# Attention output formed transposed in quadrants of 32 rows, denominator sums shared by three engines, and a new order of steps

## The chip, the cores and the metric

The kernel runs on one core of a Trainium2 chip. The metric is the device time of one execution in microseconds (us). A run more than 1.5% above the fastest of the same kernel is called slow, and only fast runs are compared. A profile gives the span, from the first instruction to the last, and this is 1.8 us shorter than the device time of the same execution, for both kernels.

## The reference, cut to what matters

A gated linear attention over 768 positions feeds a dense layer with a rational activation.

```python
# batch 4, heads 8, positions 768, head size 48; d_model 384, d_ff 2048
f = 1 / (1 + exp(-f_logit))
for t in range(S):
    state = f[t][:, None] * state + outer(k[t], v[t])
    y[t] = q[t] @ state
x = y.transpose(0, 2, 1, 3).reshape(3072, 384)      # heads side by side
h = x @ w_in                                         # 384 x 2048
P = a0 + a1*h + a2*h**2 + a3*h**3
Q = 1 + abs(b0)*abs(h) + abs(b1)*h**2
out = (P / (Q + 1e-6)) @ w_out                       # 2048 x 384
```

## The kernel before

The work is cut into 12 units of 256 rows (two batches, 128 positions). The dense part of a unit has two groups, a and b, each a tile of 128 x 2048. A list of tokens, `STEPS`, fixes the order in which the steps are put into the engines' streams; each engine's stream holds them in that order, and the traces show it kept: before, ScalarE runs `efl:4` at 63.50 us and `efl:3` behind it at 66.02, though unit 3's gates were issued first (52.2 and 58.0). `efl:3` is the gate exponential and logarithm of unit 3, `y:3` its attention output, `xe:3` the copy that leaves it as `xT` (features on partitions), `ha0:3` half of the first dense product of group a, `za`, `qa` (absolute value, square), `ua`/`Ua` the sum of the two, `La` the logarithm of the denominator, `Ea` its exponential, `ga` the quotient, `oa` and `Oa` the second product and its way out. Of the attention part, `mk` and `mq` are VectorE's products with k and q, `T` and `Te` the transposes of these and the copy that leaves them as `qkT`, `sc` the scores, `m` their mask; of the dense part, `ta` and `Ba` are VectorE's first steps of the numerator (tiles `t` and `pb`).

The attention output comes with positions on partitions, so a scaled copy and six transposes a unit stand between it and the dense product:

```python
def a_y(n):
    y = psA.tile([C, 2, 512], F32, name="y", tag="A")
    ...
    if s["c"] > 0:
        for j, p, i in heads:                        # 16 heads of the unit
            r = slice(64 * i, 64 * i + D)
            mm(j, p, i, s["qkT"][r, j, 0, p, :], s["st"][r, j, p, :])     # 48 columns
    for j, p, i in heads:
        mm(j, p, i, s["scm", j][:, i * HP + p, :], s["vn"][:, j, 2 * p + i, :])

def a_ye(n):
    nc.scalar.activation(ysb..., s["y"]..., AF.Copy, scale=sig[:, 0:1])
def a_x(n):
    for j in range(UB):
        for kk in range(KD):
            nc.tensor.transpose(xps[:, j, kk, :], s["ysb"][:, j, kk * P:(kk + 1) * P], ident)
def a_xe(n):
    nc.scalar.copy(xTs[n].rearrange("p k b t -> p b k t"), s["xps"])
```

The sum of the denominator is formed by TensorE for 22 of the 24 groups, by adding with an identity matrix, and by VectorE for two; the sums of the numerator go by accumulating DMA for 18 groups:

```python
P_BY_DMA = {4, 5, 6, ..., 21}
def m_u(n, half):                                    # tokens ua0, ua1, ub0, ub1
    for i, src in enumerate((s["h2"], s["z"])):
        for e in range(2):
            nc.tensor.matmul(u[:, e, :], ident, src[:, ...], start=(i == 0), stop=(i == 1))
def m_add_u(n):                                      # tokens Ua, Ub
    nc.vector.tensor_add(s["u"], s["z"], s["h2"])
```

The loads are issued by the sync engine and GpSimd. Two pieces of `w_in` come as fp32 through the sync queue (`wst`) and are cast by GpSimd; the rest of the weights come by GpSimd's queue. A tiny copy (`after`) makes the sync queue wait until weights have landed (9.2 us for `w_in`, 18.1 us for `w_out` before), so that loads of later units are issued after them:

```python
def load_w_in(g, dma_cast=True):
    src = moe_w_in[:, cols].rearrange("(ko ki) n -> ki ko n", ki=P)       # 128 partitions
    ...
load(0)
casts = [load_w_in(0, False), load_w_in(1, False)]
load(1)
...
def after(n):
    src = (w_in_sb[0:1, 0, d_ff - 16:d_ff], w_out_sb[0:1, KF - 1, 0:16])[n]   # the last pieces
    nc.sync.dma_start(out=hold[0:1, n, :], in_=src)
after(0)
load(2)
nc.gpsimd.tensor_copy(hold[0:1, 2, :], at_[2]["qn"][0:1, UB - 1, H - 1, 0:16])
load_v(2)
for g in range(KF // WB):
    load_w_out(g)
after(1)
for token in STEPS.split():
    ...
    if key == "mk" and n + 3 < NUN:
        load(n + 3)
```

Of the kernel before, what the change touches and what calls it, by code (L numbers as in the profile page):

```python
# [8 lines left out]
F32 = mybir.dt.float32  # L9
# [9 lines left out]
    efl:0 cs:0 A1:0 A0:0 mk:0 mq:0 T:0 sv:0 Te:0 sc0:0 m0:0 sc1:0 m1:0 y:0 al:0 ye:0 st:0 efl:1 x:0 cs:1  # L19
    xe:0 ha1:0 A1:1 A0:1 mk:1 mq:1 ha0:0 Ya1:0 Ya0:0 sv:1 T:1 ta:0 Te:1 qa:0 hb0:0 sc0:1 Yb0:0 m0:1 al:1  # L20
    hb1:0 Yb1:0 sa:0 sc1:1 m1:1 y:1 efl:2 ye:1 Bb:0 cs:2 A1:2 st:1 za:0 Ba:0 ua0:0 mk:2 A0:2 La0:0 ua1:0
    La1:0 vl:3 x:1 tb:0 mq:2 xe:1 T:2 zb:0 qb:0 ha1:1 Te:2 Ea:0 sb:0 sv:2 Pa:0 Ya1:1 ha0:1 efl:4 sc0:2
    m0:2 ub0:0 Ya0:1 efl:3 ta:1 sc1:2 al:2 hb0:1 m1:2 ga:0 Lb0:0 y:2 qa:1 Yb0:1 cs:3 A0:3 st:2 A1:3
    ub1:0 za:1 Ba:1 ye:2 Pb:0 hb1:1 x:2 Lb1:0 vl:4 Yb1:1 mk:3 qb:1 mq:3 xe:2 ha1:2 Bb:1 cs:4 Eb:0 T:3
    Ya1:2 A0:4 A1:4 ua0:1 tb:1 Te:3 zb:1 sv:3 La0:1 efl:5 sc0:3 ua1:1 sa:1 ha0:2 La1:1 Ya0:2 gb:0 oa0:0
    al:3 m0:3 sc1:3 hb0:2 sb:1 m1:3 qa:2 hb1:2 y:3 mk:4 vl:5 Ea:1 Yb0:2 Yb1:2 ub1:1 ye:3 za:2 ub0:1
    oa1:0 Lb1:1 mq:4 ta:2 Pb:1 st:3 T:4 Te:4 Lb0:1 ua0:2 Eb:1 ua1:2 sc0:4 x:3 La0:2 xe:3 Pa:1 Oa:0 m0:4
    cs:5 sv:4 La1:2 al:4 sc1:4 Ba:2 ga:1 sa:2 ob0:0 A1:5 ha0:3 m1:4 qb:2 A0:5 ha1:3 tb:2 mq:5 Ea:2 y:4
    Ya0:3 Ya1:3 Bb:2 st:4 zb:2 ye:4 efl:6 mk:5 gb:1 za:3 hb0:3 ob1:0 Yb0:3 x:4 ub1:2 T:5 hb1:3 Te:5
    Lb1:2 qa:3 Pa:2 ub0:2 Ob:0 xe:4 Yb1:3 Lb0:2 sv:5 vl:7 ha0:4 sc0:5 ta:3 al:5 Eb:2 Ba:3 Ya0:4 sb:2  # L30
    m0:5 oa0:1 ha1:4 sc1:5 ga:2 Pb:2 sa:3 ua1:3 efl:7 Ya1:4 La1:3 oa1:1 ua0:3 Oa:1 La0:3 cs:6 zb:3 m1:5
    A0:6 Pa:3 ob0:1 tb:3 qb:3 gb:2 A1:6 hb1:4 Bb:3 ob1:1 Ea:3 vl:6 Yb1:4 ub0:3 sb:3 qa:4 mk:6 y:5 Ob:1
    Ba:4 Lb0:3 ub1:3 oa0:2 cs:7 Lb1:3 mq:6 ye:5 A0:7 A1:7 za:4 hb0:4 st:5 oa1:2 T:6 ta:4 ga:3 mk:7 Te:6
    Yb0:4 Eb:3 zb:4 ua1:4 Oa:2 Pb:3 ua0:4 x:5 La1:4 mq:7 La0:4 sc0:6 ob0:2 m0:6 ob1:2 xe:5 ha1:5 Bb:4
    sv:6 sc1:6 sa:4 ha0:5 Ea:4 tb:4 qb:4 Ya1:5 al:6 ub1:4 m1:6 efl:8 sb:4 Pa:4 Ya0:5 y:6 hb0:5 Lb1:4
    gb:3 ye:6 st:6 Ob:2 hb1:5 T:7 Yb0:5 cs:8 Pb:4 za:5 ta:5 Yb1:5 x:6 A0:8 qa:5 ub0:4 oa0:3 Te:7 vl:8
    xe:6 Lb0:4 Ba:5 A1:8 oa1:3 sc0:7 Eb:4 ua1:5 ga:4 qb:5 m0:7 sa:5 ua0:5 Pa:5 Bb:5 sc1:7 La1:5 sv:7
    vl:9 La0:5 efl:9 ha0:6 al:7 m1:7 Ya0:6 ha1:6 zb:5 Ya1:6 gb:4 mq:8 Oa:3 y:7 ye:7 tb:5 hb0:6 mk:8 cs:9
    ob0:3 st:7 qa:6 T:8 Yb0:6 A0:9 hb1:6 A1:9 Ea:5 x:7 Te:8 sb:5 za:6 sc0:8 Yb1:6 vl:10 ob1:3 ta:6 ub0:5
    xe:7 m0:8 Lb0:5 Ba:6 sv:8 sa:6 mk:9 ub1:5 sc1:8 al:8 Ob:3 Lb1:5 m1:8 Pb:5 ua0:6 Pa:6 Eb:5 ga:5 oa0:4  # L40
    La0:6 ua1:6 gb:5 y:8 La1:6 mq:9 oa1:4 efl:10 qb:6 tb:6 ha1:7 zb:6 ha0:7 st:8 vl:11 Oa:4 Ya1:7 ob0:4
    ye:8 Ya0:7 sb:6 Bb:6 Pb:6 Ea:6 ub1:6 T:9 ob1:4 za:7 Lb1:6 hb1:7 Te:9 x:8 qa:7 sc0:9 Ob:4 ub0:6 Yb1:7
    ta:7 m0:9 sa:7 xe:8 hb0:7 ga:6 Lb0:6 sc1:9 cs:10 Yb0:7 oa0:5 m1:9 Ba:7 Pa:7 ua1:7 A1:10 zb:7 mk:10
    tb:7 A0:10 mq:10 qb:7 Eb:6 La1:7 ha1:8 sv:9 Ya1:8 y:9 al:9 ha0:8 ua0:7 oa1:5 ye:9 Ya0:8 gb:6 La0:7
    T:10 ub0:7 Bb:7 Oa:5 ob0:5 Te:10 za:8 Ea:7 Lb0:7 ub1:7 sb:7 efl:11 Lb1:7 sc0:10 ob1:5 Ob:5 hb1:8
    st:9 m0:10 Yb1:8 Ba:8 Eb:7 hb0:8 oa0:6 ta:8 qa:8 sc1:10 Yb0:8 cs:11 A0:11 ga:7 Pb:7 gb:7 x:9 oa1:6
    m1:10 A1:11 ua0:8 ua1:8 mk:11 xe:9 La0:8 zb:8 qb:8 y:10 La1:8 ye:10 ha0:9 sa:8 tb:8 ha1:9 mq:11 Oa:6
    Ya0:9 x:10 Ya1:9 Bb:8 ob0:6 sb:8 ta:9 za:9 ub1:8 ob1:6 Ea:8 ub0:8 Lb1:8 Lb0:8 qa:9 Pa:8 hb0:9 Yb0:9
    T:11 Pb:8 Ba:9 hb1:9 xe:10 Ob:6 Te:11 ua0:9 Yb1:9 sc0:11 Eb:8 oa0:7 sa:9 oa1:7 m0:11 La0:9 Pa:9
    ua1:9 ga:8 La1:9 sc1:11 qb:9 Oa:7 tb:9 ha1:10 Ea:9 zb:9 m1:11 ha0:10 y:11 Bb:9 Ya1:10 Ya0:10 ye:11  # L50
    ob0:7 ub0:9 sb:9 ub1:9 x:11 gb:8 Lb0:9 ta:10 ob1:7 Lb1:9 Ob:7 za:10 hb1:10 hb0:10 qa:10 oa0:8 Ba:10
    sa:10 Eb:9 ga:9 Yb1:10 Yb0:10 tb:10 ua0:10 xe:11 La0:10 ua1:10 oa1:8 La1:10 zb:10 qb:10 Oa:8 ha1:11
    Pb:9 Ya1:11 Pa:10 ha0:11 gb:9 ob0:8 ob1:8 sb:10 ub1:10 Ya0:11 Bb:10 Ea:10 za:11 Ob:8 qa:11 ub0:10
    Lb1:10 ta:11 Lb0:10 Eb:10 Pb:10 oa0:9 Ba:11 sa:11 hb1:11 Pa:11 oa1:9 hb0:11 ga:10 Yb1:11 Ua:11 Oa:9
    ob0:9 Yb0:11 ob1:9 gb:10 La0:11 qb:11 Bb:11 Ob:9 zb:11 Ea:11 Ub:11 tb:11 sb:11 ga:11 oa0:10 oa1:10
    Lb0:11 Oa:10 ob0:10 Pb:11 ob1:10 Eb:11 Ob:10 gb:11 oa0:11 oa1:11 Oa:11 ob0:11 ob1:11 Ob:11
# [3 lines left out]
P_BY_DMA = {4, 5, 6, 7, 8, 9, 10, 11, 12, 13, 14, 15, 16, 17, 18, 19, 20, 21}  # L60

TE_ON_ACT = frozenset()
O_ON_DVE = frozenset()
# [3 lines left out]
def kernel(  # L67
# [60 lines left out]
    qkp = [consts.tile([C, UB, 2, H, 64], BF16, name=f"qkp{i}") for i in range(NQK)]  # L128
    lsp = [consts.tile([C, UB, H, 64], BF16, name=f"lsp{i}") for i in range(NQK)]
    states = [consts.tile([P, UB, HP, D], BF16, name=f"state{u}") for u in range(NU)]  # L130
# [21 lines left out]
    def load_v(n):  # L152
        at_[n]["vn"] = ld.tile([C, UB, H, D], BF16, name="vn")
        rows(nc.gpsimd, at_[n]["vn"], v, n)
# [6 lines left out]

    def a_ef(n):
        s = at_[n]
        fl = "p b h d -> p (b h d)"
        ef = at.tile([C, UB, H, D], F32, name="ef")
        nc.scalar.activation(ef.rearrange(fl), s["fn"].rearrange(fl), AF.Exp, scale=-1.0)  # L166
# [17 lines left out]
    def a_mul(n, i):  # L184
        s = at_[n]
        nc.vector.tensor_mul(s["qk"][:, :, i, :, 0:D], s[("qn", "kn")[i]], s["A", i])  # L186

    def a_T(n):
        s = at_[n]
        tp = psA.tile([P, UB, 2, HP, C], BF16, name="tp", tag="A")  # L190
        for j in range(UB):
            for i in range(2):
                for p in range(HP):
                    nc.tensor.transpose(tp[:, j, i, p, :],  # L194
                                        s["qk"][:, j, i, 2 * p:2 * p + 2, :].rearrange("t h d -> t (h d)"),
                                        ident)
# [12 lines left out]
    def a_sv(n):  # L209
# [8 lines left out]
        for j in range(UB):  # L218
            for p in range(HP):
                nc.tensor.matmul(s["al"][:, j * HP + p:j * HP + p + 1],  # L220
                                 s["ls"][:, j, 2 * p:2 * p + 2, :].rearrange("t h d -> t (h d)"),
# [338 lines left out]
```

## Time and profile before

| | before |
|---|---|
| time, median of 2 runs | 268.51 us (268.48 to 268.55) |
| span of the profiled run | 265.7 us (device time 267.52) |
| busy: TensorE, VectorE, ScalarE | 229.0, 215.7, 206.5 us |
| granted TensorE clock, mean | 0.949 |
| first dense VectorE operation | 29.95 us |
| VectorE from there to its last operation | 227.5 us, of which 203.2 busy and 24.4 idle |
| tail after it | 8.2 us |

Read the table from the bottom. From its first dense operation on, VectorE has a fixed amount of work; the end moves only if that stream starts earlier, has fewer holes, or has less in it.

### The profile page before, as it was taken

How to read it: one execution, taken by the hardware profiler on the slowest of the kernel's cores; microseconds unless marked ns; L12 is line 12 of the kernel's file. 1: busy time of each engine (PE TensorE's matmuls, PEld its weight loads, DVE VectorE, ACT ScalarE, POOL GpSimd, SP SyncE). 2: the span in 40 equal slices, each digit the busy share in tenths (PEclk: the TensorE clock that was granted, in tenths of full speed). 3: DMA queues.
4: the chain of work that ended last, by engine and by line, in shares of the span. 5: the costliest groups of instructions: out<-in, count | busy, mean ns of one | idle time of the engine just before them, and what ended most of it. 6: DMA issues, size and time to landing. Idle time of an engine off the chain costs nothing.

```text
span 265.7 us, 5413 instructions
## 1 busy us (share of the span) xinstructions
PE 229.0 (86%) x2263; PEld 153.3 (58%) x2263; DVE 215.7 (81%) x237; ACT 206.5 (78%) x225; POOL 49.1 (18%) x61
## 2 busy tenths in 40 slices
PE   6659947500879999999999999999999999999884
PEld 2334726300557567666677685777667667776542
DVE  6260799300999999999999999999899889789970
ACT  3306586104999999999999998989999889989861
POOL 5080039000200022141022433211010211110000
PEclk9986997955799999999999999999999999999999
DMA  9999659999995649699999299952350852624111
GB/s 115 267 218 170 107 75 139 181 173 188 185 172 94 120 90 133 137 161 189 202 202 171 54 172 223 153 110 40 71 110 1 171 112 70 140 57 109 59 59 59
DMA packets 109975, 34.94 MB, mean 131 GB/s; under 512 B 100992, under 2 KB 106880, under 8 KB 109952
## 3 DMA queue, kind: packets, MB, share of 16 engines
q0 software_dynamic: 30464, 14.16, 42.0%
q1 hardware_dynamic: 79200, 20.45, 40.9%
q8 instruction: 17, 0.28, 0.4%
q14 instruction: 6, 0.05, 0.1%
q10 hardware_dynamic: 288, 0.00, 0.1%
HBM read 25.17 MB, written 4.72 MB: 112 GB/s over the span
## 4 chain that ended last, share of the span: by engine, by line
PE 67%; DMA 13%; SPq 7%; ACT 5%; POOL 4%; issue 2%; DVE 0%; ACTq 0%
PE hp L320 21%; PE op L419 20%; PE u L354 13%; SPq L159 7%; DMA w_in_sb<-in_moe_w_in_dram 4%; DMA w_out_sb<-in_moe_w_out_dram 3%; PE y L260 3%; PE tp L194 3%; PE sc L240 2%; DMA wst<-in_moe_w_in_dram 2%; DMA qn<-in_q_dram 2%; DMA kn<-in_k_dram 2%; ACT qi L372 1%; POOL vn L159 1%; PE xps L301 1%
## 5 line engine op out<-in xcount | busy, mean ns | idle before, releaser
L320 PE MATMUL hp<-xT,w_in_sb 128*128 128x256 bf16 x576 | 71.1, 277 | 18.4 <-ACT y L334 15.8
L320 PEld LDWEIGHTS <-w_in_sb 128*128 128x128 bf16 x576 | 56.2, 99 | 28.9 <-issue 19.0
L419 PE MATMUL op<-w_out_sb,gall 128*128 128x384 bf16 x368 | 66.2, 326 | 2.0 <-ACT osb L200 1.3
L334 ACT CAST y<-hp 128x1024 bf16<-128x1024 f32 x48 | 48.4, 1016 | 10.2 <-PE hp L320 9.7
L419 PEld LDWEIGHTS <-gall 128*128 128x128 bf16 x384 | 36.7, 98 | 26.5 <-issue 1.8
L367 ACT ACTIVATE lq<-u,sig 128x1024 f32<-128x1024 f32 x44 | 48.4, 1119 | 4.2 <-PE u L354 3.4
L372 ACT ACTIVATE qi<-lq 128x2048 bf16<-128x2048 f32 x24 | 46.2, 1925 | 0.1
L391 POOL DMA_DIRECT2D t<-pb x18 | 16.4, 910 | 134.3 <-DVE t L382 113.9
L377 DVE TENSOR_SCALAR t<-y,a_sb 128x2048 bf16<-128x2048 bf16 x24 | 20.1, 837 | 18.9 <-ACT y L334 18.8
L249 DVE TENSOR_TENSOR scm<-sc,mask 128x1024 bf16<-128x1024 f32 x24 | 29.3, 1220 | 3.4 <-PE sc L240 3.4
L402 DVE TENSOR_TENSOR gall<-t,qi 128x2048 bf16<-128x2048 bf16 x24 | 29.2, 1219 | 1.0 <-ACT qi L372 0.9
L339 DVE TENSOR_TENSOR h<-y 128x2048 bf16<-128x2048 bf16 x24 | 29.2, 1217 | 0.4 <-ACT y L334 0.4
L382 DVE TENSOR_TENSOR t<-t,h 128x2048 bf16<-128x2048 bf16 x24 | 29.2, 1218 | 0.0
L159 POOL DMA_DIRECT2D vn<-in_v_dram x24 | 23.9, 1045 | 27.4 <-PE y L260 27.4
L354 PE MATMUL u<-h,ident 128*128 128x512 bf16 x88 | 26.2, 380 | 0.6 <-ACT A L180 0.6
L354 PE MATMUL u<-z,ident 128*128 128x512 bf16 x88 | 26.2, 379 | 0.5 <-DVE z L344 0.5
L354 PEld LDWEIGHTS <-ident 128*128 128x128 bf16 x176 | 16.3, 98 | 16.9 <-issue 1.6
L166 ACT ACTIVATE ef<-fn 128x768 f32<-128x768 f32 x12 | 10.2, 854 | 19.9 <-DMA fn<-in_f_logit_dram 19.9
L180 ACT ACTIVATE A<-cs 128x768 f32<-128x768 f32 x24 | 18.4, 820 | 2.8 <-PE cs L173 2.8
L385 DVE TENSOR_SCALAR pb<-y,a_sb 128x2048 bf16<-128x2048 bf16 x24 | 20.3, 845 | 0.0
L186 DVE TENSOR_TENSOR qkp<-kn,A 128x768 bf16<-128x768 f32 x12 | 11.4, 951 | 10.1 <-ACT A L180 7.0
L344 DVE TENSOR_SCALAR z<-y 128x2048 uint16<-128x2048 uint16 x24 | 17.3, 721 | 0.9 <-ACT y L334 0.9
(59 smaller groups left out, 226.8 us busy)
## 6 DMA issues: line engine op xcount, KB each, us to landing
t<-pb POOLq DMA_DIRECT2D x18, 512.0 KB, 5.3
fn<-in_f_logit_dram SPq DMA_DIRECT2D x24, 192.0 KB, 4.4
kn<-in_k_dram SPq DMA_DIRECT2D x24, 192.0 KB, 4.6
qn<-in_q_dram SPq DMA_DIRECT2D x24, 192.0 KB, 4.9
out_dram<-osb SPq DMA_DIRECT2D x24, 192.0 KB, 2.0
vn<-in_v_dram POOLq DMA_DIRECT2D x24, 96.0 KB, 5.7
wst<-in_moe_w_in_dram SPq DMA_DIRECT2D x2, 768.0 KB, 6.1
w_out_sb<-in_moe_w_out_dram POOLq DMA_DIRECT2D x4, 384.0 KB, 7.5
```

What stands on the lines that cost most here:

```text
L159: eng.dma_start(out=dst[:, j], in_=src[u * UB + j, :, c * C:(c + 1) * C, :].rearrange("h t d -> t h d"))
L249: nc.vector.tensor_mul(m, s["sc", j].rearrange("s i p t -> s (i p) t"), mb)
L320: nc.tensor.matmul(hp[:, e, :], w_in_sb[:, kk, f * P:(f + 1) * P], xT[:, kk, :], start=(kk == 0), stop=(kk == KD - 1))
L334: nc.scalar.copy(part_of(tile_of(n, "y"), half), mg[n]["hp", half].rearrange("p a n -> p (a n)"))
L339: nc.vector.tensor_mul(s["h2"], s["y"], s["y"])
L354: nc.tensor.matmul(u[:, e, :], ident, src[:, (half * 2 + e) * NB:(half * 2 + e + 1) * NB], start=(i == 0), stop=(i == 1))
L367: nc.scalar.activation(lq if whole else part_of(lq, half), s["u"] if whole else s["u", half].rearrange("p a n -> p (a n)"), AF.Ln, scale=s ...
L372: nc.scalar.activation(part_of(tile_of(n, "qi"), part, parts), part_of(mg[n]["lq"], part, parts), AF.Exp, scale=-1.0)
L382: nc.vector.tensor_mul(s["t"], s["t"], s["h2"])
L385: nc.vector.tensor_scalar(tile_of(n, "pb"), mg[n]["y"], a_sb[:, 1:2], a_sb[:, 0:1], op0=ALU.mult, op1=ALU.add)
L402: nc.vector.tensor_mul(galls[m][:, lo:lo + w, :].rearrange("p a n -> p (a n)"), part_of(s["t"], part, parts), part_of(s["qi"], part, parts))
L419: nc.tensor.matmul(ops[m, b], galls[m][:, mm, b * C:(b + 1) * C], w_out_sb[:, mm, :], start=(mm == 0), stop=(mm == KF - 1))
```

## The change

The intent: form the attention output already transposed, so that the copy `ysb` and the transposes `x` go; take the sums of the denominator off TensorE, mostly to accumulating DMA; give eight copies of `qkT` to ScalarE in exchange; and search a new order that knows how long the first loads take.

Each matmul of the new output writes into one quadrant of 32 rows. Two heads of 48 rows fill three quadrants, and the middle one gets 16 rows of each. Heads 0 to 3 go to partitions 0 to 63 and heads 4 to 7 to partitions 64 to 127. The rows of `xT` thereby stand in another order than the features of the reference, and the rows of `w_in` must stand in the same one; each piece of `w_in` is therefore loaded by two transfers of 64 partitions.

```diff
 # attention output: features on partitions, in quadrants
-        y = psA.tile([C, 2, 512], F32, name="y", tag="A")
+        y = psA.tile([P, KD, UB, C], F32, name="y", tag="A")
+        cols = {(1, 1): (0, 32), (0, 0): (ZC, ZC + 32), (1, 2): (32, 64), (0, 1): (ZC + 32, 64)}
+        def mm(j, p, i, quad, lhsT, rhs):
+            lo, hi = cols[p % 2, quad]
+            qd = 3 * (p // 2) + quad
+            r = 64 * i + 32 * (qd % 2)
+            nc.tensor.matmul(y[r:r + hi - lo, qd // 2, j, :], lhsT[:, lo:hi], rhs, ...)
+        todo = [(j, p, i, quad) for j in range(UB) for half, quad in cols
+                for p in range(half, HP, 2) for i in range(2)]
...
-    def a_ye(n):
-    def a_x(n):
 def a_xe(n):
-        nc.scalar.copy(xTs[n].rearrange("p k b t -> p b k t"), s["xps"])
+        nc.scalar.activation(xTs[n], s["y"], AF.Copy, scale=sig[:, 0:1])
 # sums
-P_BY_DMA = {4, 5, 6, ..., 21}                                # 18
+P_BY_DMA = {5, 7, 8, 10, 11, 13, ..., 20, 21, 22}             # 15
+U_BY_DMA = {3, 7, 8, 9, 10, 12, 13, 14, 17, 19, 21, 23}       # 12; 6 on TensorE, 6 on VectorE
-TE_ON_ACT = frozenset()
-O_ON_DVE = frozenset()
+TE_ON_ACT = {0, 1, 2, 4, 5, 7, 8, 11}
+O_ON_DVE = {(4, 0), (10, 0)}
 def m_add_u(n):
+        if n in U_BY_DMA:
+            nc.gpsimd.dma_start(out=s["u"], in_=s["h2"], accum_op=ALU.add)
 # loads of the head
-        src = moe_w_in[:, cols].rearrange("(ko ki) n -> ki ko n", ki=P)
+        src = [moe_w_in[i * DM // 2:(i + 1) * DM // 2, cols].rearrange("(ko ki) n -> ki ko n", ki=P // 2)
+               for i in range(2)]
...
-            nc.sync.dma_start(out=t, in_=src)
+            for i in range(2):
+                nc.sync.dma_start(out=t[i * P // 2:(i + 1) * P // 2], in_=src[i])
...
+    for t in vpd + states:
+        nc.gpsimd.memset(...)                                 # five tiles
-        src = (w_in_sb[0:1, 0, d_ff - 16:d_ff], w_out_sb[0:1, KF - 1, 0:16])[n]
+        src = (w_in_sb[0:1, 0, 3 * WB * P - 16:3 * WB * P], w_out_sb[0:1, 3 * WB - 1, 0:16])[n]
-    nc.gpsimd.tensor_copy(hold[0:1, 2, :], at_[2]["qn"]...)
+    nc.gpsimd.tensor_copy(hold[0:1, 2, :], at_[2]["kn"]...)
 # order: all of STEPS is new; in the first lines
-    ... sc0:0 m0:0 sc1:0 m1:0 y:0 al:0 ye:0 st:0 efl:1 x:0 cs:1 xe:0 ha1:0 ... efl:4 sc0:2 ... efl:3 ...
+    ... sc0:0 m0:0 efl:1 sc1:0 m1:0 y:0 xe:0 st:0 cs:1 A0:1 A1:1 ha0:0 mk:1 mq:1 ha1:0 ... za:0 ... efl:3 ... efl:4 ...
```

The layouts of the tiles that hold q, k, the gates, v and the state were changed to fit; loads of unit n + 3 now wait in program order for the third of the three reads of unit n. The diff also has fewer dummy matmuls on zeros, which keep TensorE busy in the head: 31 for 47.

## The prediction

> **What bounds the kernel now.** I read the slices of the page first. The columns are 40 equal slices of 6.64 us; the digits are tenths busy, and PEclk is the granted clock.
>
> ```profile
> PE   6659947500879999999999999999999999999884
> DVE  6260799300999999999999999999899889789970
> ACT  3306586104999999999999998989999889989861
> PEclk9986997955799999999999999999999999999999
> ```
>
> Three regimes show: a head in which all engines are part idle, a hole in slices 9 and 10 (53 to 66 us) in which TensorE and VectorE are at 0 and the clock falls to 0.5, and a long middle with every engine at 9. Next the list of waits over the whole run (total us, times, longest), and the sync engine's own:
>
> ```profile
> ACT ef L166 <- DMA fn<-in_f_logit_dram: 19.9, 2, 16.3
> DVE t L377 <- ACT y L334: 18.8, 3, 16.2
> PE hp L320 <- ACT y L334: 15.8, 1, 15.8
> SPq L492 <- DMA w_out_sb<-in_moe_w_out_dram: 18.1, 1, 18.1
> ```
>
> The first three are one event. The timeline of that place gives its cause (start us, length us):
>
> ```profile
> 51.63 0.50 SPq L492 DMA_DIRECT2D hold<-w_out_sb  x1
> 52.23 2.26 SPq L159 DMA_DIRECT2D fn<-in_f_logit_dram  x2
> ...
> 58.03 1.75 SPq L159 DMA_DIRECT2D fn<-in_f_logit_dram  x2
> ...
> 63.50 0.84 ACT L166 ACTIVATE ef<-fn 128x768 f32<-128x768 f32 x1 [16.28 <-DMA fn<-in_f_logit_dram]
> ...
> 66.17 2.72 PE L320 MATMUL hp<-xT,w_in_sb 128*128 128x256 bf16 x12 [15.80 <-ACT y L334]
> ```
>
> The sync queue issues in order. It stands on "after(1)", a tiny copy that waits for the last piece of w_out, until 51.6; only then come the loads of unit 3 (52.2) and unit 4 (58.0). And the order has `efl:4` ahead of `efl:3`, so ScalarE waits for the later of the two, and with it everything else. Then the stretches (us, busy of each engine, clock, DMA share, GB/s) say what binds once the stream runs:
>
> ```profile
> 110.00:150.00 40.00, 40.00 (x417) 26.61 (x412) 40.00 (x43) 38.15 (x43) 8.67 (x10) 1.00 0.97 156
> 150.00:190.00 40.00, 40.00 (x458) 28.54 (x457) 38.91 (x43) 37.73 (x44) 10.31 (x11) 1.00 0.87 132
> 190.00:230.00 40.00, 40.00 (x372) 27.04 (x370) 37.64 (x40) 36.89 (x38) 5.12 (x6) 1.00 0.44 96
> ```
>
> TensorE is at 40.00 of 40, VectorE at 94 to 100%, ScalarE at 92 to 95%. Two engines bind together, so relieving TensorE alone is worth only what VectorE leaves idle: 40.00 − 37.64 = 2.4 us of the last window. I take VectorE as the measure: its first operation of the dense stage is at 29.95 (`ta:0`), its last at 257.47, which is 227.5 us. It is busy 215.66 − 12.55 (before 30 us) = 203.1 of them and idle 24.4: 16.2 in the hole, 8.2 elsewhere. 265.7 − 257.5 = 8.2 us of tail follow.
>
> [...] 16 transposes with 128 columns advance the chain by 0.89 us, 56 ns each; 32 y matmuls with 48 columns by 0.81 us, 25 ns each. [...] In the trace two row tiles do run side by side: 8 score matmuls of 128 columns span 0.40 us, of which one alone takes 0.218, so 26 ns a step against 56. Quadrants of 32 columns are not in this trace. [...]
>
> **The change part by part.** The durations are from these groups (busy us, mean ns):
>
> ```profile
> L354 PE MATMUL u<-h,ident 128*128 128x512 bf16 x88 | 26.2, 380 | 0.6 <-ACT A L180 0.6
> L393 DVE TENSOR_TENSOR t<-t,pb 128x2048 bf16<-128x2048 bf16 x6 | 7.3, 1218 | 0.0
> L200 DVE COPY qkT<-tp 128x2048 bf16<-128x2048 bf16 x12 | 14.7, 1222 | 3.9 <-PE tp L194 3.9
> L276 ACT ACTIVATE ysb<-y,sig 128x768 bf16<-128x768 f32 x12 | 11.0, 914 | 5.5 <-PE y L260 5.5
> L367 ACT ACTIVATE lq<-z,sig 128x2048 f32<-128x2048 bf16 x2 | 4.0, 2006 | 0.0
> ```
>
> *TensorE.* The identity sums u fall from 22 groups to 6. One group is 8 matmuls of 512 columns, 8 × 0.216 = 1.73 us in the chain (4 take 0.86), so −16 × 1.73 = −27.7 us. The 72 transposes x go: 72 × 56 ns = −4.0. The new y has 64 matmuls of 128 columns a unit (32 in the two first units) for 32 of 48 columns: at the 25 ns [...], 704 instead of 352, +8.8 us. Sum −22.9. Without any overlap they would cost 56 ns, +30, and the sum would be −1.
>
> *VectorE.* Sums u on it: 2 to 6, +4 × 1.22 = +4.9. Sums of t and pb on it: 6 to 9, +3.7. Eight of the twelve qkT copies leave: −9.8. Two output copies come, about 0.5 each (the 384-element state product takes 0.552): +1. Sum −0.2: nothing.
>
> *ScalarE.* [...] The twelve ysb go: −11.0; xT now reads fp32 with a pointer, 0.914 for 0.814: +1.2. Logarithms: 12 halves at 1.119 and 18 whole at 2.006 for 44 and 2: −3.7. Two output copies: −1.0. Sum +0.6 on 206.5.
>
> *DMA.* Twelve sums u and 15 of t: 27 accumulating transfers of 512 KB for 18. From 190 to 240 us, with no loads, the share sums to 21.9 us of all engines for 7 of them and the output stores, so at most 3.1 us each; nine more are at most 28 us over some 170, or 0.16 on a share of 0.9.
>
> *The head.* Both holds now wait for the third piece of four, and the one on GpSimd for kn instead of qn. I estimate the w_in hold 2 us sooner (27.8 to about 25.5), the kn gate another 2, and one piece of w_out, a fourth of the 11.5 us from 40.1 to 51.6, 2.9: unit 3's loads issue about 45 instead of 52.2, and fn is there 4.4 us later, near 50. Its reader is now the right one, `efl:3`, and comes later: by my count in program order 34.5 us of ScalarE work stand before it, against 22.6 before the old `efl:4`. With xT of unit 0 at 21.5 to 22 and 27.5 us of ScalarE work from there (× 0.94, as successive durations overlap: summed durations 218.9, busy 206), ScalarE cannot be there before 47.5, and VectorE (25.9 us of work in the same order, × 0.93, from 26.5) comes to that place at 50.6. So the hole shrinks to 0 to 3 us. Unit 0 itself loses the ysb step and the transposes: before, y ends at 20.1, xT at 24.1, the first hp is at 25.6. Without ysb and x (3.2 us), [...] hp starts near 22.5 and the first dense VectorE operation (`za:0`) near 26.5 instead of 29.95. It matters because VectorE has one unbroken stream from there.
>
> *Sum.* Start 26.5; VectorE work 203.1 × (220.4 ÷ 219.4 of summed durations left) = 204; idle 9, of which 2 while few jobs are ready, 4 in the middle and 3 at the end, where the last sum u (`Ub:11`) goes by DMA and ScalarE then does logarithm, exponential in series; tail 8.2. Span 247.7. Timed runs lie 2.8 over the span (268.5 − 265.7): 250.5. I call it 251.
>
> **The rivals.**
> 1. *The hole moves rather than closes.* If the loads of units 3 and 4 still come late (GpSimd now clears five tiles before it loads v of unit 0, and issues two more descriptor batches of 0.77 us each for w_in), 3 to 8 us of idle stay: 254 to 259. For it: the chain of waits runs through these very DMAs for its first 65 us. Against it: the order was searched with load times.
> 2. *DMA becomes the bound.* Share already reaches 1.49 between 73 and 80 us; a sum that took 5.3 us (4.5 to 7.3) may take 10, and ScalarE's logarithm now waits for it. Worth 0 to 8 us: up to 259. Against it: shares over 1 in the old middle cost VectorE nothing.
> 3. *The y quadrants run one after another.* Then TensorE is where it was (−1 us), still with VectorE at its side: the middle keeps its 6 us of idle, and I get 254. So this mechanism hardly decides the time.
> 4. *Better than said.* TensorE no longer binding, the idle of 180 to 250 us goes fully and the tail tightens: 245 to 247.
>
> **Range and chances.** The sum is 251; a closed hole and an unbroken middle make 246, one of the first three rivals 254 to 259, two of them 262. I give 245 to 259 8 times in 10. Same would need 263 or more, which needs the hole back in most of its size: 0.03. Slower would need the new transfers to break the middle: 0.01.
>
> **What would show it.** Right: ScalarE's wait for fn under 4 us in one piece; no empty slice after the fourth; first z near 26.5; VectorE busy 213 to 218, ScalarE 204 to 211; TensorE under 82% of the span, 48 u matmuls left in place of 176, y matmuls some 25 ns apart or less. Wrong: a wait over 5 us on fn, kn or w_out; a wait of the logarithm on an accumulating DMA over 3 us in total; landing times of sums above 8 us; VectorE idle over 6 us in the middle; VectorE busy above 220.

## The result, and the profile after

| | before | after |
|---|---|---|
| time, median of 2 runs | 268.51 us | 253.78 us (253.5 to 254.06) |
| span of the profiled run | 265.7 | 252.3 |
| mean granted clock | 0.949 | 0.946 |
| busy: TensorE, VectorE, ScalarE | 229.0, 215.7, 206.5 | 207.8, 213.6, 207.6 |
| first dense VectorE operation | 29.95 | 33.77 |
| VectorE busy, idle from there to its last operation | 203.2, 24.4 | 202.3, 7.9 |
| tail | 8.2 | 8.35 |

The ratio is 0.9451, with a 95% interval of 0.9406 to 0.9497. A ratio here is the mean time of one kernel's fast runs over the mean of the other's fast runs of the same rounds, so it is not quite the ratio of the medians that are quoted. The kernel is faster by 5.5%. The span is 1.8 us shorter than the device time of the same execution, for both kernels.

First the slices of the kernel after, columns as in the prediction, 6.31 us each:

```profile
PE   8667366946988898887998969989999999997754
DVE  7122168899999999999999999979999999999940
ACT  2425427799899999998996999998999899999841
PEclk9977959795897999999999999999999999999999
```

No slice is empty any more, and the hole at slices 9 and 10 is gone. But in slices 5 and 6 VectorE is at 1 and 6 tenths, where before it was at 7 and 9: it comes into its stream later. The waits over the whole run (total us, times, longest) say the same:

```profile
ACT ef L174 <- DMA fn<-in_f_logit_dram: 8.5, 2, 4.7
DVE qkp L197 <- DMA qn<-in_q_dram: 8.5, 2, 6.0
...
ACT lq L372 <- DMA z<-h: 5.0, 7, 1.9
SPq L502 <- DMA w_out_sb<-in_moe_w_out_dram: 12.9, 1, 12.9
```

The wait for the gates fell from 19.9 to 8.5 us. In both kernels 3.6 to 3.7 us of it is the very first load. The wait of 16.28 for unit 4 is gone entirely: in the timeline `efl:3` runs at 60.89 and `efl:4` at 72.05, both with no wait. New are a wait of 4.74 for the gates of unit 1, VectorE's wait for q, 6.0 us at its longest, and the logarithm's seven waits for sums that DMA now forms. VectorE too waits for these transfers, 1.7 us in all before `h`, 1.5 before `gall` and 0.8 before `pb`: 4.0 of the 7.9 us that it is idle in its stream, where before it had no such wait. The timeline of the head shows where the waits for gates and q stand (start us, length us):

```profile
21.87 0.84 ACT L174 ACTIVATE ef<-fn 128x768 f32<-128x768 f32 x1 [4.74 <-DMA fn<-in_f_logit_dram]
23.49 0.88 ACT L309 ACTIVATE xT<-y,sig 128x768 bf16<-128x768 f32 x1
...
32.90 0.96 DVE L197 TENSOR_TENSOR qkp<-qn,A 128x768 bf16<-128x768 f32 x1 [5.96 <-DMA qn<-in_q_dram]
33.77 0.68 DVE L346 TENSOR_SCALAR z<-y 128x2048 uint16<-128x2048 uint16 x1
```

`efl:1` stands before `xe:0` in ScalarE's stream, so `xT` of unit 0 waits for the gates of unit 1. The product with q of unit 1 stands before `za:0` in VectorE's stream, and its load lands at 32.9; before, that product began at 28.11. Traffic in this part fell. The stretch from 8 to 16 us, before and then after (busy of TensorE, weight load, VectorE, ScalarE and GpSimd with their instructions, clock, DMA share, GB/s):

```profile
8.00:16.00 8.00, 6.77 (x71) 3.68 (x70) 3.14 (x3) 1.63 (x3) 2.91 (x3) 1.00 1.19 288
```

```profile
8.00:16.00 8.00, 5.91 (x54) 3.70 (x53) 1.92 (x2) 2.43 (x4) 0.00 (x0) 0.83 1.29 194
```

The DMA engines are as busy (share 1.29 for 1.19; the profile's figure can exceed 1) and move a third less. Then the middle and the end, in the same columns; the first fence is of before, the second of after:

```profile
180.00:240.00 60.00, 60.00 (x569) 40.85 (x564) 54.13 (x59) 55.56 (x57) 7.14 (x8) 1.00 0.41 89
```

```profile
110.00:180.00 70.00, 63.54 (x801) 45.27 (x790) 68.09 (x74) 65.86 (x65) 17.89 (x18) 1.00 1.00 165
180.00:240.00 60.00, 56.12 (x602) 38.51 (x600) 59.00 (x65) 56.66 (x53) 13.24 (x15) 1.00 0.75 144
```

Before, TensorE was busy throughout from 180 to 240 and VectorE idled 5.9 us; now TensorE has 3.9 us of slack and VectorE idles 1.0. From 110 to 180, before had 70.00 of TensorE and 69.85 of VectorE. The sums that moved show in the traffic, 144 GB/s for 89.

The accounts of after minus before, along VectorE: idle −16.5, first dense operation +3.8, work −0.9, tail +0.1, together some −13.4 us, which is the difference of the spans. So the change won 16.5 us of holes and paid back 3.8 in the head.

### The profile page after: what moved, and what is told of

It reads as the page before. It is cut to its first block, busy times and chain, and to the rows that moved or that the text cites. A ratio compares the mean times of both kernels' runs of the same rounds, so it can differ in the third digit from the quotient of the medians.

```text
span 252.3 us, 5762 instructions
## 1 busy us (share of the span) xinstructions
PE 207.8 (82%) x2423; PEld 142.1 (56%) x2423; DVE 213.6 (85%) x238; ACT 207.6 (82%) x203; POOL 60.4 (24%) x77
## 4 chain that ended last, share of the span: by engine, by line
DVE 27%; DMA 25%; PE 14%; ACT 13%; issue 10%; SPq 9%; POOL 1%; DVEq 0%; POOLq 0%; ACTq 0%
DMA z<-h 9%; DMA t<-pb 8%; SPq L163 7%; PE hp L322 6%; DVE gall L407 5%; DMA qn<-in_q_dram 4%; DVE h L341 4%; PE op L424 4%; ACT y L336 4%; DVE scm L260 4%; DVE qkp L197 3%; DMA fn<-in_f_logit_dram 3%; ACT qi L377 3%; ACT lq L372 2%; DVE t L387 2%
## 5 line engine op out<-in xcount | busy, mean ns | idle before, releaser
L424 PE MATMUL op<-w_out_sb,gall 128*128 128x384 bf16 x368 | 67.1, 331 | 6.5 <-ACT osb L212 4.2
L372 ACT ACTIVATE lq<-z,sig 128x2048 f32<-128x2048 bf16 x18 | 36.2, 2011 | 5.1 <-DMA z<-h 5.0
L364 POOL DMA_DIRECT2D z<-h x12 | 12.1, 1005 | 76.4 <-ACT A L190 25.4
L396 POOL DMA_DIRECT2D t<-pb x15 | 14.8, 990 | 61.0 <-DVE t L387 56.1
L163 POOL DMA_DIRECT2D vpd<-in_v_dram x24 | 24.8, 1139 | 13.6 <-PE cs L182 13.5
L212 ACT COPY qkT<-tp 128x2048 bf16<-128x2048 bf16 x8 | 15.1, 1884 | 11.6 <-PE tp L206 11.6
L206 PE MATMUL tp<-ident,qkp 128*128 128x128 bf16 x192 | 14.5, 235 | 10.7 <-DVE qkp L197 10.0
L390 DVE TENSOR_SCALAR pb<-y,a_sb 128x2048 bf16<-128x2048 bf16 x24 | 19.3, 805 | 1.8 <-ACT y L336 1.0
L206 PEld LDWEIGHTS <-qkp 128*128 128x128 bf16 x192 | 12.9, 106 | 13.1 <-DVE qkp L197 12.0
L197 DVE TENSOR_TENSOR qkp<-qn,A 128x768 bf16<-128x768 f32 x12 | 11.4, 950 | 8.5 <-DMA qn<-in_q_dram 8.5
```

What stands on the lines that cost most here:

```text
L163: eng.dma_start(out=dst[:, j], in_=src[u * UB + j, :, c * C:(c + 1) * C, :].rearrange("h t d -> t h d"))
L197: nc.vector.tensor_mul(paired(s["qk"][:, i]), s[("qn", "kn")[i]].rearrange(nat, i=2), s["A", i].rearrange(nat, i=2))
L206: nc.tensor.transpose(tp[:, j, i, p, :], s["qk"][:, i, p, j].rearrange("t i d -> t (i d)"), ident)
L372: nc.scalar.activation(lq if whole else part_of(lq, half), s["u"] if whole else s["u", half].rearrange("p a n -> p (a n)"), AF.Ln, scale=s ...
L424: nc.tensor.matmul(ops[m, b], galls[m][:, mm, b * C:(b + 1) * C], w_out_sb[:, mm, :], start=(mm == 0), stop=(mm == KF - 1))
```

## The experiments

Three questions are asked: what made the head later, what closed the hole, and what binds in the middle. Experiments without "before" in their name change the kernel after; those with it change the kernel before.

### The head: e1_whole

If the halves of `w_in` are the reason, then loading the pieces by one transfer of 128 partitions must bring the head back. The rows are then in the wrong order, so the result is wrong (relative error 0.029); the instructions and the amount of data are the same.

```diff
-        src = [moe_w_in[i * DM // 2:(i + 1) * DM // 2, cols].rearrange("(ko ki) n -> ki ko n", ki=P // 2)
-               for i in range(2)]
+        src = moe_w_in[:, cols].rearrange("(ko ki) n -> ki ko n", ki=P)
-            for i in range(2):
-                nc.sync.dma_start(out=t[i * P // 2:(i + 1) * P // 2], in_=src[i])
+            nc.sync.dma_start(out=t, in_=src)
 # and the same for the pieces on GpSimd's queue
```

> The changed kernel, but each piece of w_in is loaded by one transfer over all 128 partitions instead of two over 64 (the output is wrong on purpose: the rows no longer fit the new order of xT). Theory: the halves of 64 partitions are what makes the head late[...]; then from 8 to 16 us the traffic is above 250 GB/s as in the kernel before (288 there, 195 in the changed one), q of unit 1 has landed by 29 us instead of 32.9, the first dense VectorE operation is at 29 to 30 instead of 33.8 and the time falls by 3 to 5 us, to 249 to 251. Rival: the head is late from the cleared tiles on GpSimd, the copy on ScalarE or the order; then the first z stays within 1 us of 33.8 and the time within 1 us of 253.8.

Measured: 248.6 us (248.38 to 250.26, four runs), ratio 0.9274 [0.9206, 0.9341]. The stretch from 8 to 16 us of this kernel, and its timeline at the start of the stream:

```profile
8.00:16.00 8.00, 5.33 (x62) 2.96 (x61) 1.92 (x2) 3.38 (x4) 2.58 (x3) 1.00 1.31 281
```

```profile
20.21 0.90 ACT L309 ACTIVATE xT<-y,sig 128x768 bf16<-128x768 f32 x1 [0.79 <-PE y L277]
...
22.42 4.05 PE L322 MATMUL hp<-xT,w_in_sb 128*128 128x256 bf16 x24
...
28.20 0.96 DVE L197 TENSOR_TENSOR qkp<-qn,A 128x768 bf16<-128x768 f32 x1 [3.03 <-DMA qn<-in_q_dram]
29.07 0.68 DVE L346 TENSOR_SCALAR z<-y 128x2048 uint16<-128x2048 uint16 x1
```

Traffic is back at 281 GB/s, q of unit 1 comes 4.7 us sooner, and the whole kernel is 1.8 points, some 5 us, faster. Along VectorE, against after: first dense operation −4.7, idle −2.2, work −0.3, tail +1.8 (its last but one group of op matmuls took 4.46 us for 2.77), which gives −5.4, the difference of the spans (246.9 and 252.3). The halves are the larger part of the lost head; the fewer dummy matmuls can't be that part, as this kernel has them too. Even so the first dense operation is at 29.07 and not at the predicted 26.5. Two other marks of the prediction are met here, though: hp starts at 22.42 (22.5 predicted; 24.43 in after), and the gates of unit 3 are issued at 44.35 (45; 49.2 in after). The gates of unit 1 no longer hold up `xT`: their wait is 2.27 us for 4.74, and `xT` waits for y instead.

### The head, from the other side: e3_before_half

The reverse, on the kernel before: halves in place of whole pieces, again wrong.

```diff
-        src = moe_w_in[:, cols].rearrange("(ko ki) n -> ki ko n", ki=P)
+        src = [moe_w_in[i * DM // 2:(i + 1) * DM // 2, cols].rearrange("(ko ki) n -> ki ko n", ki=P // 2)
+               for i in range(2)]
 # each piece by two transfers
```

> The kernel before, but each piece of w_in is loaded by two transfers over 64 partitions (wrong output on purpose): the one part of the change that I suspect of the late head, alone. Theory: q of unit 1 lands at 31 to 33 us instead of 28.1, the chain of holds after it shifts, and as the hole at 53 to 66 us hangs on that chain the time grows by 3 to 5 us, to 271.5 to 273.5. Rival: within 1 us of 268.5.

Measured: 270.67 us (269.99 to 270.91) against 267.98 of before, ratio 1.0075 [1.0021, 1.0129]. The product with q of unit 1 begins at 32.04 for 28.11, and traffic from 8 to 16 us is 207 GB/s for 288. The direction is as expected, and q is delayed by 3.9 us where the change has 4.8, but only 2.0 us (by the ratio; 0.6 to 3.5 by its interval) reach the end, less than the 3 to 5 expected. The hole does not take up the difference: it is as long as before (16.4 us), ends 3.1 us later (66.56 for 63.50), and the profiled run's span is 3.4 us longer. A profiled run can lie more than 1 us off the median, so the size stays uncertain.

### Why a half is slow: m1_ports

A kernel of loads alone (its output is zeros). Each stage moves 1.57 MB of `w_in`, in four transfers of 64 partitions or two of 128, and then VectorE reads a bit of each tile; each stage runs twice.

```diff
+        stage("low", [(sp, 0, halves[g][0]) for g in range(4)])      # partitions 0 to 63
+        stage("high", [(sp, 64, halves[g][1]) for g in range(4)])    # 64 to 127
+        stage("mid", [(sp, 32, halves[g][0]) for g in range(4)])     # 32 to 95
+        stage("whole", [(sp, None, whole[g]) for g in range(2)])     # 0 to 127
+        stage("alt", [(sp, 64 * i, halves[g][i]) for g in range(2) for i in range(2)])
+        stage("two", [((sp, act)[i], 64 * i, halves[g][i]) for g in range(2) for i in range(2)])
```

> No attention at all: only loads of w_in's fp32 pieces, the output is zeros on purpose. Six stages, twice, of 1.57 MB each with the same 2 KB runs: four transfers to partitions 0 to 63; four to 64 to 127; four to 32 to 95; two over all 128; low and high half in turn on the sync queue; low on the sync queue beside high on ScalarE's. [...] low and high take 1.5 to 2 times as long as 32 to 95, which is as fast as all 128; two queues are fast, in turn on one queue is slow or between. Rival, number of partitions or of transfers: 32 to 95 is as slow as low and high. Rival, neither: all stages are within 10%, and the late head comes from the loads beside it.

The timeline has for each stage its issue on the sync queue and the read that waited for the last landing; the lines of the first low, mid and whole stage:

```profile
0.72 2.71 SPq L39 DMA_DIRECT2D wlow<-in_moe_w_in_dram  x4
...
11.63 0.37 DVE L43 COPY acc<-wlow 64x16 f32<-64x16 f32 x2 [1.56 <-DMA wlow<-in_moe_w_in_dram]
...
22.83 2.58 SPq L39 DMA_DIRECT2D wmid<-in_moe_w_in_dram  x4
...
30.57 0.75 DVE L43 COPY acc<-wmid 32x16 f32<-32x16 f32 x4 [0.58 <-DMA wmid<-in_moe_w_in_dram]
31.34 0.94 SPq L39 DMA_DIRECT2D wwhole<-in_moe_w_in_dram  x2
...
37.98 0.39 DVE L43 COPY acc<-wwhole 128x16 f32<-128x16 f32 x2 [6.66 <-DMA wwhole<-in_moe_w_in_dram]
```

| stage | issue to last landing, first and second time, us |
|---|---|
| low, 0 to 63 | 10.9, 10.6 |
| high, 64 to 127 | 10.4, 10.2 |
| mid, 32 to 95 | 7.7, 8.3 |
| whole, 0 to 127 | 6.6, 6.6 |
| low and high in turn, one queue | 10.25, 10.15 |

The same number of transfers of the same size takes 10.9 us on partitions 0 to 63 and 7.7 on 32 to 95. So between these two the number of descriptors or transfers is not the reason; which partitions they reach is. What it is in these partitions that does it, the runs do not show. The measured ratio of low to whole is 1.6. Expected was a mid stage as fast as the whole; it takes 1.1 to 1.7 us longer, with twice as many transfers, and what that is due to stays open. With two queues, the two transfers on the sync queue took 8.1 us for three of the four (one on ScalarE's queue had begun earlier), about the same time a byte as in turn on one queue: three quarters of 10.2 are 7.7. The expectation that two queues are fast has failed.

### Repairing the head: e2_twoq and e11_poolq

Both keep the halves and are correct. The first issues the upper half of the two fp32 pieces from ScalarE's queue.

```diff
-                nc.sync.dma_start(out=t[i * P // 2:(i + 1) * P // 2], in_=src[i])
+                (nc.sync, nc.scalar)[i].dma_start(out=t[i * P // 2:(i + 1) * P // 2], in_=src[i])
```

> The changed kernel with a right result: of the first two pieces of w_in the lower half is still issued on the sync queue, the upper half on ScalarE's queue, [...]. Theory [...]: the casts on GpSimd start 2 to 3 us sooner (16.0 and 19.7 before), q of unit 1 lands 2 to 3 us sooner, time 251 to 252. Rival (the number of descriptors or the issue on the queue is the limit, or HBM is): less than 1 us of the head moves, time within 1 us of 253.8. ScalarE's own issue costs it some 1.2 us of an idle stretch.

Measured: 251.63 us (250.25 to 254.69, three fast and one slow run), ratio 0.9353 [0.9289, 0.9417]. The time is what the theory asked for, the way there is not: traffic from 8 to 16 us is 164 GB/s, less than in after (194), the casts of the two pieces come at 18.39 and 21.56, and q of unit 0 is delayed from 12.32 to 16.45. Only q of unit 1 comes sooner, at 30.67 for 32.90, and the first dense operation at 32.36. The 1.2 us expected for ScalarE's issue are an estimate, which fits the sync queue in after: 0.61 us (median) for one of these halves. Against after, the idle of VectorE falls by 2.3 and its start by 1.4. Why that pays for the later unit 0 stays open.

The second issues the upper halves from GpSimd's queue, at about 6 us, ahead of its casts.

```diff
-            for i in range(2):
-                nc.sync.dma_start(out=t[i * P // 2:(i + 1) * P // 2], in_=src[i])
+            nc.sync.dma_start(out=t[0:P // 2], in_=src[0])
+            return (lambda: nc.gpsimd.dma_start(out=t[P // 2:P], in_=src[1]), ...)
...
+    for upper, _ in casts:
+        upper()
```

> The changed kernel with a right result; the upper halves of the first two pieces of w_in are issued by GpSimd at some 6 us, beside the lower halves on the sync queue, and not as early as ScalarE's queue did (there they got ahead of k and q of unit 0, whose product came at 16.5 us instead of 12.3). Theory: [...] traffic from 8 to 16 us rises from 194 to over 240 GB/s, the casts start near 14 and 17, q of unit 1 lands at 29 to 30, time 249 to 251. Rival: the sharing does not help (two queues gave 164 GB/s), time 251.5 to 254.

Measured: 251.86 us (250.95 to 252.75, four runs), ratio 0.9391 [0.9346, 0.9436]. Traffic from 8 to 16 us is 206 GB/s, the casts come at 17.25 and 20.44, the first dense operation at 31.16. The gain is small, as the rival had it: two queues do not make the halves a whole (281 GB/s in e1_whole).

### A layout with a third in one transfer: e13_third

If the quadrants are assigned so that the middle third of `w_in` is again one transfer of 128 partitions, only two thirds come in halves. This is correct.

```diff
+            kk = ((0, 2, 1), (1, 0, 2))[i][qd // 2]
-            nc.tensor.matmul(y[r:r + hi - lo, qd // 2, j, :], lhsT[:, lo:hi], rhs,
+            nc.tensor.matmul(y[r:r + hi - lo, kk, j, :], lhsT[:, lo:hi], rhs,
...
+            nc.sync.dma_start(out=t[:, 1], in_=middle)
+            nc.sync.dma_start(out=t[0:P // 2, 0:KD:2], in_=ends[0])
 # the other end by GpSimd, as in e11_poolq
```

> The best version that keeps the result right: the changed kernel with another assignment of the quadrants to the three blocks of xT, so that the middle 128 rows of each piece of w_in lie in 128 partitions in order and come by one transfer over all of them; only the other two thirds still come in halves of 64 partitions, the upper half of the first two pieces issued by GpSimd beside the lower one on the sync queue. Whole pieces (wrong result) gave 248.6, ratio 0.927 to the kernel before; halves on two queues gave 251.6 and 251.9, ratios 0.935 and 0.939. [...] a third of the loss comes back on top of the two queues, q of unit 1 lands at 29 to 30, 249.5 to 251, ratio 0.930 to 0.936. Rival, [...]: 252 or more, ratio 0.940 and up.

Measured: 255.05 us median of seven runs, of which only two were fast (251.54 and 250.31), ratio of the fast runs 0.9377 [0.9325, 0.9429]. The profile fell in a slow run, so its times are not compared with others. The interval covers that of e11_poolq almost wholly. This run does not show a gain; it is inconclusive.

### Is the first dense operation the right mark? e12_reorder

The prediction let the stream begin with the first dense operation. Here 20 tokens of the head are put in another order, so that `za`, `Ba`, `ta` and `qa` of unit 0 come before q of unit 1.

```diff
-    A0:1 A1:1 ha0:0 mk:1 mq:1 ha1:0 T:1 Ya0:0 sv:1 Ya1:0 za:0 hb0:0 Te:1 Ba:0 sc0:1 ta:0 hb1:0 Yb0:0
-    qa:0 Yb1:0 m0:1 ...
+    A0:1 A1:1 ha0:0 mk:1 ha1:0 Ya0:0 Ya1:0 za:0 Ba:0 ta:0 qa:0 mq:1 T:1 sv:1 hb0:0 Te:1 sc0:1 hb1:0 Yb0:0
+    Yb1:0 m0:1 ...
```

> The changed kernel with twenty tokens of the head in another order, nothing else: VectorE does z, pb, t and h of group 0 before the product with q of unit 1, behind which they stood; the result stays right. In the changed kernel y of group 0 is ready at 28.3 us, but z waits until 33.8, as q of unit 1 lands at 32.9 and VectorE takes its work in order. Theory: these four operations (3.6 us) fill the wait, the rest of the stream comes 3 us sooner, time 250 to 251. Rival: what follows needs q of unit 1 anyway, or the loads, and under 1 us is won.

Measured: 255.7 us (252.63 to 257.94, two fast and two slow runs), ratio of the fast runs 0.9481 [0.9416, 0.9546]: no gain. VectorE's timeline in this kernel:

```profile
27.92 0.69 DVE L346 TENSOR_SCALAR z<-y 128x2048 uint16<-128x2048 uint16 x1 [1.61 <-ACT y L336]
...
32.01 0.96 DVE L197 TENSOR_TENSOR qkp<-qn,A 128x768 bf16<-128x768 f32 x1 [0.82 <-DMA qn<-in_q_dram]
...
38.14 1.23 DVE L260 TENSOR_TENSOR scm<-sc,mask 128x1024 bf16<-128x1024 f32 x1 [5.17 <-PE sc L251]
```

The dense operation now runs at 27.92, in a time that was idle, and 5.17 us of idle appear before the mask of unit 1. The rival holds. I read it so: the chain from q of unit 1 through its transposes, copy and scores starts the unbroken stream, and it starts with a load. The profiled run, one of the two fast ones, has a span of 250.9 us, 1.4 below after, so a gain of about 1 us isn't excluded.

### What closed the hole: e4_before_swap and e5_before_swap_gates

The first exchanges `efl:4` and `efl:3` in the old order and does nothing else.

```diff
-    ... Ya1:1 ha0:1 efl:4 sc0:2 m0:2 ub0:0 Ya0:1 efl:3 ta:1 ...
+    ... Ya1:1 ha0:1 efl:3 sc0:2 m0:2 ub0:0 Ya0:1 efl:4 ta:1 ...
```

> The kernel before with two tokens of the order exchanged, so that the gates of unit 3 come before those of unit 4; nothing else. The f of unit 3 is issued at 52.2 us against 58.0, so ScalarE's wait should end near 57 instead of 63.5. Theory: most of the gain of the change is the hole, so this alone gives 5 to 7 us, to 261.5 to 263.5. Rival: the work behind the gates of unit 4 then waits in its turn for k and q of unit 3 or for unit 4, and under 3 us are won.

Measured: 264.69 us (263.92 to 266.3), ratio 0.9864 [0.9802, 0.9926], some 3.5 us won. The wait for the gates shrinks from 16.3 to 11.85 us, and a second of 3.3 appears behind it. Together that is 15.2, so the waits fell by little: the exchange divides the wait more than it removes it. The gain lies between theory and rival. Where it comes from is not shown: along VectorE, the profiled run has its first dense operation 1.1 us sooner, which the exchange doesn't touch, 0.9 less idle and 0.6 less work.

The second does the exchange and takes the new gates of the change: both holds wait for the third piece of four, and GpSimd's for k.

```diff
+    (the exchange of e4_before_swap)
-        src = (w_in_sb[0:1, 0, d_ff - 16:d_ff], w_out_sb[0:1, KF - 1, 0:16])[n]
+        src = (w_in_sb[0:1, 0, 3 * WB * P - 16:3 * WB * P], w_out_sb[0:1, 3 * WB - 1, 0:16])[n]
-    nc.gpsimd.tensor_copy(hold[0:1, 2, :], at_[2]["qn"]...)
+    nc.gpsimd.tensor_copy(hold[0:1, 2, :], at_[2]["kn"]...)
```

> The kernel before with the exchanged tokens and with the new gates (third piece of w_in and w_out, k instead of q): the part of the change that deals with load times, without any new arithmetic. The exchange alone gave 264.7 and left a wait of 11.9 us on f of unit 3. Theory: unit 3 is issued 4 to 7 us sooner, the wait shrinks to 5 to 8 us, time 259 to 261. Rival: the gates only let the loads crowd each other and under 1 us is won.

Measured: 260.5 us (259.87 to 261.83), ratio 0.9719 [0.9672, 0.9767]. The wait in this kernel (total us, times, longest; the first load of all is one of the three):

```profile
ACT ef L166 <- DMA fn<-in_f_logit_dram: 14.4, 3, 7.0
```

Two edits of the head, without any of the new arithmetic, give 2.8 of the change's 5.5 points, about half; VectorE's idle falls by 6.3 us (24.4 to 18.1). The wait is not gone: 7.04 and 3.89 us remain for units 3 and 4, where the change has none. The rest of its order and of its moved work does that; which part does it, these runs do not separate.

### What binds in the middle: e7_u_dve and e6_u_pe

First the twelve sums that go by DMA are given to VectorE.

```diff
-U_BY_DMA = {3, 7, 8, 9, 10, 12, 13, 14, 17, 19, 21, 23}
+U_BY_DMA = set()
```

> The changed kernel with the twelve sums u of the DMA put on VectorE. If VectorE sets the time, as my prediction had it, each costs 1.13 us (start to start), 13.6 in all, less what of its 8 us of idle goes: 261 to 267. If the accumulating transfers themselves cost as much in waits as they save, the time is within 3 us of 253.8.

Measured: 263.52 us (262.95 to 266.51), ratio 0.9863 [0.9788, 0.9937]. VectorE's work in its stream rises by 13.2 us (202.3 to 215.5) and its idle falls from 7.9 to 3.9; the span rises by 8.6. Work put on VectorE comes out at the end, less what its idle could take. VectorE sets the time, and the transfers are worth their place, though they cost it waits: of the 4.0 us that VectorE waits for accumulating transfers in after, 0.3 are left here.

Then all sums are given back to TensorE, within the new order, each just ahead of its logarithm.

```diff
-    ... Ua:0 ... La0:0 ... Ub:0 ... Lb0:0 ...
+    ... ua0:0 La0:0 ua1:0 La1:0 ... ub0:0 Lb0:0 ub1:0 Lb1:0 ...
 # and so for all groups that were on VectorE or DMA
```

> The changed kernel with all sums u on TensorE as in the kernel before (18 groups by 8 matmuls of 512 columns, 31 us of TensorE work; in four places a step of the order had to come earlier so that two PSUM buffers are enough). It takes six sums from VectorE and twelve from the DMA. My prediction: TensorE then binds again beside VectorE (208 + 31 = 239 of 252 us busy), VectorE has 7 us less, so between -3 and +4 us of 253.8. Rival, relieving TensorE is what the change lives on: +8 us or more, 262 and up.

Measured: 309.2 us (308.01 to 310.37), ratio 1.1555 [1.1505, 1.1604]. The wait that makes it:

```profile
ACT lq L374 <- PE u L358: 46.3, 27, 4.6
```

TensorE is busy 243.9 us of 307.7, so it isn't full. The time is far beyond both theory and rival. The logarithm waits 27 times; I put this down to the sums' late place in TensorE's stream, behind dense products that wait for other engines. The sum waits in its turn 14 times, 17.3 us in all, for the logarithm, as I read it to free one of two PSUM buffers (TensorE's accumulators). This kernel shows what a badly placed sum costs, not what TensorE's relief is worth. That question stays open.

### The quadrants: e9_y_serial

In the change, successive y matmuls go to different quadrants. Here they are sorted so that all of one quadrant come first.

```diff
-        todo = [(j, p, i, quad) for j in range(UB) for half, quad in cols
-                for p in range(half, HP, 2) for i in range(2)]
+        todo = sorted(((j, p, i, quad) for j in range(UB) for half, quad in cols
+                       for p in range(half, HP, 2) for i in range(2)),
+                      key=lambda t: (t[2], (3 * (t[1] // 2) + t[3]) % 2))
```

> The changed kernel with the y matmuls sorted by quadrant, so that neighbours write the same 32 rows[...]. The trace of the changed kernel has 64 of them in 1.12 us of the chain. Sorted they should take 56 ns each, 3.6 us a unit, 27 us more of TensorE in all. Prediction's third rival: about +3 us, 255 to 258, as TensorE has the room. If the y step is on the path of each unit, up to 2.5 us x 12 = 30 us, 265 and up.

Measured: 256.63 us (255.55 to 258.1, four runs), ratio 0.9604 [0.9548, 0.9661], that is 1.5 points or some 4 us over after (2.9 by the medians). The two passes of 32 in one unit, first of after, then of this kernel:

```profile
125.33 0.63 PE L277 MATMUL y<-qkT,state 48*32 48x128 bf16 x32
125.89 0.63 PE L277 MATMUL y<-scm,vpd 128*32 128x128 bf16 x32
```

```profile
110.48 1.34 PE L277 MATMUL y<-qkT,state 48*32 48x128 bf16 x32
111.75 1.34 PE L277 MATMUL y<-scm,vpd 128*32 128x128 bf16 x32
```

A pass advances TensorE's chain by 0.56 us in after and 1.27 here: 17.5 and 40 ns a matmul, where one alone takes 226 to 236 ns (the means of its forms in after). TensorE is busy 218.5 us for 207.8, and ScalarE's copy of `xT` waits 8.3 us in all for y. So matmuls of 128 columns in four quadrants do run side by side: 32 of them end within 0.63 us. The sort put them only partly in series, at 40 and not at the expected 56 ns, and TensorE rose by 10.7 us and not by 27: the 3 to 4 us are the worth of this part alone. The third rival of the prediction, with no overlap at all, gave 3.

## Why the prediction was right or wrong

The time, 253.78, lies in the range and 2.8 over the predicted 251. The sum by its own terms, in us:

| term | predicted | measured | difference |
|---|---|---|---|
| first dense VectorE operation | 26.5 | 33.8 | +7.3 |
| VectorE's work from there | 204 | 202.3 | −1.7 |
| idle | 9 | 7.9 | −1.1 |
| tail | 8.2 | 8.35 | +0.15 |
| span | 247.7 | 252.3 | +4.6 |
| timed run less span | 2.8 | 1.5 | −1.3 |

**The hole: right.** No wait is left for the gates of units 3 and 4. The cause was as read: with exchange and gates alone (e5_before_swap_gates) half of the gain is there. Unit 3's gates were issued at 49.2 and not at 45; with whole pieces (e1_whole) it is 44.35, so this is the delay of the halves again. It did not matter, for ScalarE came to them at 60.9, where I had put 47.5 at the earliest. In e1_whole it came at 53.85 and did not wait either, so the hole is not closed by the late head alone. The mark "under 4 us in one piece" is still missed, by the 4.74 us for unit 1, which is a matter of the head.

**VectorE's work: right.** It is busy 213.6 us in all (213 to 218 predicted), ScalarE 207.6 (207), TensorE 207.8, which is 21.2 less for 22.9 predicted. ScalarE's predicted sum of +0.6 counts +15.1 us for the eight qkT copies, which no trace of before showed on ScalarE; in after they are 1.884 us each, 15.1 in all. TensorE's agreement is in part luck: with y at its measured 17.5 ns the prediction's own sum would be −28.2 (−27.7 − 4.0 + 704 × 17.5 ns − 8.8), so the terms aren't confirmed by the total. e7_u_dve shows that VectorE was rightly taken as the measure. TensorE's share, 82.4%, is at the mark "under 82%" and not under it.

**The middle: right.** VectorE idles 1.9 us of 70 and 1.0 of 60 there.

**The head: the step that failed.** It is the sentence that hp "starts near 22.5 and the first dense VectorE operation (`za:0`) near 26.5". I followed only the data of that operation (y, xT, hp) and not what stands before it in the engines' streams. Three things were in the diff, and I did not add them up. First, `w_in` in halves: I counted two more descriptor batches for it but no slower transfer. q of unit 1 is delayed by 4.7 us by this (e1_whole; 3.9 in e3_before_half), and m1_ports shows that a half is slow in itself (10.2 to 10.9 us for 6.6 whole). Second, `mq:1` is ahead of `za:0` in VectorE's stream, so that load holds up the dense operation: in e1_whole the data of `za:0` are ready at 27.51 (the last copy of y), and it begins at 29.07, right behind q. That is 1.6 of the other 2.6 us. The remaining 1.0 is in the data: hp starts on time there, but its 24 matmuls take 4.05 us from 22.42 (2.87 from 24.43 in after). The granted clock was 0.64 there from 16 to 24 us, and 1.00 in after from 24 to 28. Third, `efl:1` is ahead of `xe:0` in ScalarE's, which makes `xT` of unit 0 wait 4.74 us; it is finished at 24.4 where I had 22. With whole pieces it is finished at 21.1, so most of this too is the late load of the halves.

**"One unbroken stream from there": wrong.** e12_reorder had its first dense operation at 27.92, and no gain. What starts the stream is, as I read that run, q of unit 1 and the chain behind it. The table's first line measures the head only because in both kernels the first dense operation (`ta:0` before, `za:0` after) happens to stand close to that chain.

**The sums by DMA: right in time, and beyond a mark.** I had said that a logarithm waiting over 3 us for accumulating DMAs would be wrong; it waits 5.0, in seven pieces of at most 1.9, while ScalarE has slack. The landing times after (KB each, median us) support that they became slower:

```profile
t<-pb POOLq DMA_DIRECT2D x15, 512.0 KB, 6.1
z<-h POOLq DMA_DIRECT2D x12, 512.0 KB, 6.1
```

The median was 5.3 before (4.5 to 7.3); single ones reach 8.1. The second rival, DMA as the bound, is there in small (in before, at a share of 1.39 from 120 to 130 us, VectorE was busy all 10.00): half of the idle that VectorE has left in its stream (4.0 of 7.9 us) is waiting for these transfers. The w_out hold waits 12.9 us for 18.1 and GpSimd's hold 13.6 us for kn, also over the mark of 5; but the gates of units 3 and 4 behind them come before they are wanted, so this mark was badly chosen.

**The quadrants: right, with a size off.** I took 25 ns a matmul; it is 17.5. The old trace was read too simply: 0.81 us for 32 y matmuls runs to the end of the last one. The first 16, in two row tiles, start 0.30 us ahead of the second 16 (99.92 and 100.22 us), 19 ns each, so some 25 ns was the pace of the second pass alone (26 ns each, to the next matmul at 100.64). The weight loads between them add no cost that shows: in after a load of 32 columns takes 96 to 102 ns, one of 128 columns 98 to 100 (`gall`, `w_in_sb`), and a load and a matmul together advance the chain by 17.5 ns.

**From span to time.** The 2.8 us compared the timed median with the span of another run. The profiled run of before took 267.52 us for its span of 265.7, so the offset is 1.8, and it is 1.8 in after too. Of the −1.3 in the table, −1.0 is this, and −0.3 is that the median of after lies 0.28 below its profiled run.

The prediction came so near by luck, as two errors of opposite sign met: the head was 7.3 us too early, and work, idle and offset were 4.1 us too high together.

Two versions are faster than both kernels by their medians and correct: e2_twoq (251.63 us) and e11_poolq (251.86). Their intervals touch that of the change, which was timed in other rounds, so "about 0.6 to 1 point" is as far as it goes. The 248.6 of e1_whole shows what a layout with whole transfers would be worth; a correct kernel with it was not found. The natural order of the rows was not run; I took it for unsafe, which no run shows.

## What to carry to other kernels

Before you say when an operation starts, list what is ahead of it in its own engine's stream, and for each of these the load that it waits for; the data path of the operation alone gave 26.5 us here, and 33.8 was measured. A new layout that looks free on the engines can be paid for in the load: look at which partitions a transfer reaches, not only at its bytes (in m1_ports 1.57 MB took 10.2 to 10.9 us on either half, 7.7 and 8.3 on partitions 32 to 95, 6.6 on all 128). Moving work from one engine to transfers paid here, where the engine that it left sets the time: with the twelve sums put back on VectorE the time was 263.52 us for 253.78 (e7_u_dve).
